# An order of TensorE's work searched anew, with six planning constants and two buffer counts changed

## The chip, the core and the metric

The kernel runs on one core of a Trainium2 chip. A core has a matmul engine (TensorE, PE in the profile, its weight loads shown apart as PEld), a vector engine (VectorE, DVE), an activation engine (ScalarE, ACT), a general one (GpSimd, POOL) and one that issues transfers (SyncE, SP). They run side by side and wait for each other through semaphores. PE writes its results into PSUM, which has eight banks of 128 x 512 fp32 values; VectorE or ScalarE must read a bank out before PE may fill it again. The metric is the time of one execution on the device, in microseconds (us); less is better.

## What is computed

```python
def reference(A_x, A_wq, A_wk, A_wv, A_wo, B_x, B_w_gate, B_w_up, B_w_down, gate_w):
    def _A_ref(x, wq, wk, wv, wo):
        q = (x @ wq).reshape(B, S, H, Dh).transpose(0, 2, 1, 3)
        k, v = x @ wk, x @ wv
        scores = jnp.einsum("bhqd,bkd->bhqk", q, k) * (Dh ** -0.5)
        o = jnp.einsum("bhqk,bkd->bhqd", _softmax(scores), v)
        return o.transpose(0, 2, 1, 3).reshape(B, S, H * Dh) @ wo
    def _B_ref(x, w_gate, w_up, w_down):
        return (_sigmoid(x @ w_gate) * (x @ w_up)) @ w_down
    x = A_x
    g = _sigmoid((x * gate_w).sum(-1, keepdims=True))
    return g * _A_ref(x, ...) + (1 - g) * _B_ref(x, ...)
```

S is 2048 positions, D 512, 32 heads of 16 that share one key and one value head, F 1792. Everything is fp32; products that need the accuracy are made from a high and a low part of each operand, three matmuls for one.

## The kernel before

The 2048 queries are four blocks of 512. A *unit* is four heads of one block: 32 units. For each unit PE computes scores twice. First for the largest score of every query (`maximum`, L1139, code m): the result fills a bank and VectorE reduces it to its maximum (L1141). When a unit's maxima are done, they are turned by a small matmul (T, `max_turn`, L998) and sent into spare rows of the query tile, so that the second computation of the scores (`scores`, L1148, code s) comes out with the maximum taken off; ScalarE takes the exponential (L1150) into a tile `p`. Four such tiles are a *chunk* of 128 keys, and `pv` (L1012, code V) multiplies them with the values into a bank that gathers the unit's sums. The gated layer and the output projections are filled in between, as *fills* (`fill`, L1113, code f): gate, up and down products of the four blocks, then the projection of the attention's results.

Scores and fills contract over 64 rows or fewer, so PE runs two of them at once, one on each half of the array: a *step* is such a pair. V, T and the first projections (G, `project`, L870) use PE in another shape, so the work is a row of steps with *visits* to the other shape between them.

What PE does, in which order, is written out in the string `ORDER` (L683 to L728). Each letter is one code, taken by `State.step` (L657). `V`, `G` and `T` are as above. A hexadecimal digit is a step: its upper two bits say what the upper half gets, its lower two what the lower half gets (0 nothing, 1 a maximum, 2 a score, 3 a fill), so `f` is two fills, `5` two maxima, `b` a score and a fill, `c` a fill alone. A dot issues nothing; it lets the plan's clock run by 25 units. `plan()` (L731) walks through the string and lists all instructions of all engines in order; nothing of its clock reaches the chip, but it decides which engine takes which result, when transfers are issued, and which bank each product gets.

`State` books costs in units. A step is 100, a chunk `VALUES` = 371, a change into the other shape `IN`, out of it `OUT`. A bank that VectorE reads is booked as free `LATE` (until VectorE can begin) + `RED` (a reduction) + `TAIL` + `FREE` units after its matmul (`issue_m`, L514); one that ScalarE reads, `LATE_A` + `EXP` + `TAIL_A` + `FREE_A` (`issue_s`, L524). `take` (L189) hands out the bank that has been free longest and demands that it is free by the plan's clock. At the end of a visit inside a unit the sums' bank is copied out by ScalarE (`finish`, L1016); the first copy of a unit stays, later ones are added to it by GpSimd (`add_sums`, L1025).

`PB` is the number of `p` tiles (2 KB per partition each; the plan lets no more than `PB` wait for their chunk, `can_s`, L509, though `step` itself doesn't ask), `DB` that of tiles for split down weights and output weights (`wd`, 4 KB per partition each, two for one transferred pair). GpSimd splits them (L771, L772) as soon as a pair is free.

After the string comes a fixed end (L1169 to L1197): the last unit's sums are copied out, turned, divided, turned back, multiplied by the last output weights and stored.

Of the kernel before, what the change touches and what calls it, by code (L numbers as in the profile page):

```python
# [118 lines left out]
class State:  # L121
# [559 lines left out]


ORDER = (  # L683
    "GGGGGGG555G55G555.G55........5G55GG555GGG555G55G555GG55G557G777fddfffdffdfd7GT7dffff7ffd75Gdefffdfe7edef6f6f9fbf"
    "7b7b7bbdfedef97bf9fbffeeaaVV555VVV7b7b7bfbdedbdbf9fededededbf7bfb76fef67effd9VVVV5b7b7bfbfe7eeddbf6fedeedef7f6fe"
    "7bdbdbf6fbf5VTVV555VVVV7b7bb7fedbdbde7bfededeedef7e7fedb7bbd7bffd6V569VV97fbdbb7f9fe7ef6fbdededee7fb7f6f9fb7edef"
    "f75VVV59aVV97fbe7dbfbdbf6f9fbdededee7fe7f9f9fbdffd7775VVTVV655VVV76fef97efedee7f6f9fb7b7bbdfdbfb7edbdbfefed5VV56"
    "6VVV5bfbf97bf6fbf9f9fededeedef77e7bfb7be7ffddd5VVVV7b7bb7b7fededef9fe7edeede7ff6f9fe7e7bf9fbfaTV5a5VVVV5bbb77fef"
    "9fbdef6dbfedeede7f7efe7edb7eff7775VV599VV595VVV5eeedfbdf6fb7edbfbdb7bb7bdff97bfef9fe7edfd5VV566VVVdededefe7e7e7b"
    "dbfb7b7b7bbdfedf6feedf9ff7775VTVV596VV9dfbf6bdfb7bdbf9ef7ededee7ff6fed6febffb7bb9V555VVVVV5e9ffef6fbdef6e7bdfb7b"  # L690
    "7bbdfedfb79feed7bffd6V695VV569VV5a5VTVdedeedfe7e7e7bbdfb7b7b7bbfddbfbd6fede7efbfaV599VV5bb7fbb7fe7eedf9f6fededee"
    "f7b7fed6fe7dfd7777VVV599VV5ededefefb7e7e7bfbdb7b7bbdfedf9fbede7ff75f5VVVV966V5efeedbfb77b7bfedbddd7TVV999V9b77bf"
    "fededeedb7fefbb5VV566VV695VV5bfbf6f9f6fbde7b7efededee7fedbf76fbbdbfdbf5VV659TVV5eedfe7bfe7bf6dedbfb7b7bbfdf6f9f9"
    "fef6fedf75VVVVVVV7b7bbddef9fb7e7efbdeeeded7ffe7bf6fede7b7f5bV995VV5bbfbd7efb7bdef9fe7ededee7ff6fbdb7ebdf7ff56VVV"
    "TVVde5eefbdfb7afd7bfed7b7bbbfd7bedf6fedefb7fd6V595VVVVV7bdef9f6fb7ef97bfbdedeede7f7bf6f9fee7fbdbfaV5aaVV569VV959"
    "VV97bfb7f6f9feb7defe7edeede7ff6bfde7efb5bffa7TVV59aVVVVVV5efbf6defedb7b7edefb7bb7bfdf9fb7bdeedf6ff5dVVV5bb7bfb7f"
    "bd6fef9fededeeddfb7bbf76fef6fbfee6V9a9VV5a9VVVV5b7bbfefdb7af7defbdedeede7fb7f6fb7bf6fed9fdV555VVTVV97b7bff6f9fb7"
    "eedf6fedeede7ff67bfedefe7f7776VV999VVVV9dfeed7bfb7eededfb7b7b7bbdfedfb79fef6def7f5VVV555VVVdedeedfe7e7bf97efb7bb"
    "7b7bdf7bfb7b7eeeddfdddVTVVV5bbfdbf6f9fb7bf9efdeddeedbfb7b7fe7e7beffed5VVVV7b7b7bfededb7bf9fedededee7f7bf6fbb7f6d"
    "effd5VVV566VV5eefdef6fbdbf97ef9fb7b7bbfddbfe7b7bdefedbddTVV665VV569VV5b7bbff6fedef97bf6fdedeeef77efbde7bf9fe77d7"  # L700
    "VVVVVV5efededbfb7ef9f6fe7b7b7bbfddeedf9fef9fb7bfaV569VV699VVV5bb7fef6fede7ededbfb7bb7bfd7ebdf6fef9fbdfe5V566VV95"
    "6TVV595VVV79b7bfdef9fb7be7fededeedef77ee7f9fbbdf6fbfaV656VVV5efedbf9f9fbf6f6edfb7bb7bfdf9efde7bb7fdfdd5VV665VVVT"
    "V7b7bdbdef6fbf9edbf7ededee7ff67bfedefefb797bVVVdedefe7b7b7b7bfbdeefd5VV6ddefefb7b7b7bf9fefed9VVVVVV7b7edbdbfe7ed"
# [543 lines left out]
```

## Time and profile before

| | |
|---|---|
| median of 3 runs | 1588.13 us (1587.35 to 1588.98) |
| the profiled execution, its own time | 1589.17 us |
| its span, first to last instruction | 1587.0 us |
| mean granted TensorE clock | 0.999 |
| reductions on VectorE (L1141) | 2048, 1256.0 us busy |
| exponentials on ScalarE (L1150) | 2048, 1035.4 us busy |
| splits and additions on GpSimd, all | 788.7 us busy |
| bytes moved | 102.04 MB, mean 64 GB/s |

Rows of groups give line, engine, operation, output and inputs, shapes and the count, then the busy time, the mean length of one in ns, and the idle time of the engine before them with what ended it. Rows of the timeline and of the chain give the start and the length in us; neighbouring instructions of one kind are merged, so a length covers all of them. Matmuls overlap, so their starts tell more than their lengths. Each V leaves eight records on L1012: four matmuls, each shown twice.

### The profile page before, as it was taken

The page shows a single profiled execution, that of the slowest core. Times are in us where ns is not written, and L with a number is a line of the kernel's source. Part 1 is how long each engine was busy: PE and PEld are TensorE (multiplying, and loading weights), DVE is VectorE, ACT ScalarE, POOL GpSimd, SP SyncE. Part 2 cuts the span into 40 slices and gives each one's busy share as a digit, 9 for nine tenths or more (in the row PEclk, how much of TensorE's full clock was granted, in tenths as well). Part 3 has the DMA queues.
Part 4 walks back from the last instruction along what each step waited for, and adds up shares of the span by engine and source line. Part 5 has one row for each costly group of instructions (what it writes and reads, how often), then busy time and mean ns, then how long its engine had stood idle before and what let it go on. Part 6 is the DMA issues. An engine that isn't in the chain of part 4 may idle for free.

```text
span 1587.0 us, 33642 instructions
## 1 busy us (share of the span) xinstructions
PE 1578.4 (99%) x12950; PEld 1026.2 (65%) x12950; DVE 1357.7 (86%) x2320; ACT 1233.2 (78%) x2426; POOL 788.7 (50%) x662
## 2 busy tenths in 40 slices
PE   9999999999999999999999999999999999999998
PEld 7776666666666566666656666666666666676663
DVE  6989999999888889898998889888998988888751
ACT  4277787888778877887877978888887877787887
POOL 4253373657363455376463537274726346436432
PEclk9999999999999999999999999999999999999999
DMA  7422021122021221122121212022212122112011
GB/s 248 159 80 65 25 78 31 50 78 79 25 78 39 82 75 52 34 72 65 43 75 41 80 50 83 27 63 65 78 35 75 39 75 78 52 35 62 15 35 51
DMA packets 56000, 102.04 MB, mean 64 GB/s; under 512 B 16612, under 2 KB 18148, under 8 KB 55840
## 3 DMA queue, kind: packets, MB, share of 16 engines
q1 hardware_dynamic: 55840, 99.89, 20.3%
q8 instruction: 102, 1.67, 0.5%
q14 instruction: 58, 0.48, 0.1%
HBM read 78.11 MB, written 21.22 MB: 63 GB/s over the span
## 4 chain that ended last, share of the span: by engine, by line
PE 95%; ACT 3%; DVE 1%; SPq 0%; DMA 0%; issue 0%; POOL 0%; DVEq 0%; ACTq 0%
PE bank L1113 32%; PE bank L1012 29%; PE bank L1139 17%; PE bank L1148 14%; PE bank L870 3%; ACT p L1150 2%; SPq L986 0%; PE bank L998 0%; DVE mx L1141 0%; PE bank L1191 0%; DMA qs<-qd 0%; ACT x L796 0%; DVE x L802 0%; DMA wkv_raw<-wkv 0%; ACT q L965 0%
## 5 line engine op out<-in xcount | busy, mean ns | idle before, releaser
L1141 DVE TENSOR_REDUCE mx<-bank 128x1 f32<-128x512 f32 x2048 | 1256.0, 683 | 163.1 <-PE bank L1139 136.5
L1150 ACT ACTIVATE p<-bank 128x512 f32<-128x512 f32 x2048 | 1035.4, 665 | 4.9 <-PE bank L1148 1.0
L1148 PE MATMUL bank<-qs,ks 64*128 64x512 f32 x2048 | 725.8, 396 | 0.0
L1139 PE MATMUL bank<-ks,qs 62*128 62x512 f32 x2048 | 674.6, 409 | 0.2 <-DMA qs<-qd 0.2
L1012 PE MATMUL bank<-p,v_aug 128*32 128x512 f32 x4096 | 486.7, 597 | 0.3 <-ACT p L1150 0.3
L1139 PEld LDWEIGHTS bank<-ks,qs 62*128 62x128 f32 x2048 | 334.5, 184 | 152.7 <-issue 51.9
L1148 PEld LDWEIGHTS bank<-qs,ks 64*128 64x128 f32 x2048 | 361.9, 185 | 77.1 <-ACT p L1150 31.2
L1026 POOL TENSOR_TENSOR ou<-ou,ou 128x512 f32<-128x512 f32 x181 | 233.3, 1290 | 283.8 <-ACT ou L1019 277.2
L1019 ACT COPY ou<-bank 128x512 f32<-128x512 f32 x212 | 129.7, 612 | 279.4 <-PE bank L1012 136.5
L1113 PE MATMUL bank<-x,wu 64*128 64x512 f32 x1344 | 272.1, 391 | 0.3 <-SPq L1117 0.3
L1012 PEld LDWEIGHTS bank<-p,v_aug 128*32 128x32 f32 x4096 | 122.4, 109 | 230.1 <-issue 192.4
L1113 PE MATMUL bank<-wd,hl 64*128 64x512 f32 x1344 | 271.0, 391 | 0.0
L1113 PE MATMUL bank<-x,wg 64*128 64x512 f32 x1344 | 269.2, 391 | 0.0
L1113 PEld LDWEIGHTS bank<-x,wu 64*128 64x128 f32 x1344 | 201.5, 185 | 18.3 <-issue 1.7
L1113 PEld LDWEIGHTS bank<-wd,hl 64*128 64x128 f32 x1344 | 200.3, 185 | 17.0 <-issue 0.8
L1113 PEld LDWEIGHTS bank<-x,wg 64*128 64x128 f32 x1344 | 199.4, 185 | 16.8 <-issue 1.2
L845 POOL CAST wg<-rg 128x1024 fp32r<-128x1024 f32 x27 | 28.1, 1039 | 137.8 <-PE bank L1113 64.2
L1092 POOL TENSOR_TENSOR ba<-ba,pa_d 128x512 f32<-128x512 f32 x29 | 36.8, 1282 | 83.8 <-ACT pa_d L1089 83.8
L845 POOL CAST wu<-ru 128x1024 fp32r<-128x1024 f32 x27 | 28.1, 1041 | 97.8 <-PE bank L1113 58.1
L772 POOL TENSOR_TENSOR wd<-rd,wd 128x512 fp32r<-128x512 f32 x56 | 72.3, 1291 | 4.5
L772 POOL TENSOR_TENSOR hl<-h,hl 128x512 fp32r<-128x512 f32 x56 | 72.0, 1286 | 4.5
L1113 PE MATMUL bank<-wa,o 64*128 64x512 f32 x360 | 70.0, 392 | 0.0
(82 smaller groups left out, 758.4 us busy)
## 6 DMA issues: line engine op xcount, KB each, us to landing
rg<-wg SPq DMA_DIRECT2D x28, 512.0 KB
ru<-wu SPq DMA_DIRECT2D x28, 512.0 KB
rd<-wd SPq DMA_DIRECT2D x28, 512.0 KB
qs<-qd SPq DMA_DIRECT2D x192, 64.0 KB
qd<-q SPq DMA_DIRECT2D x32, 256.0 KB
od<-ou SPq DMA_DIRECT2D x31, 256.0 KB
xf<-x_in SPq DMA_DIRECT2D x16, 256.0 KB
ra<-wo SPq DMA_DIRECT2D x8, 512.0 KB
```

What stands on the lines that cost most here:

```text
L772: lo.tensor_tensor(hl[:, 1, :], raw, f32(hl[:, 0, :]), op=ALU.subtract)
L845: nc.gpsimd.tensor_copy(WS[item][:, 0, :], raw)
L870: nc.tensor.matmul(ps, w[:, p, part(kc)], X[b, kc][:, q, :], start=i == 0, stop=i == 3 * KC - 1)
L1012: nc.tensor.matmul(ps[32 * j:32 * j + 32, :], v_aug[:, c, :], PT.pop((u, c, j)), start=start, stop=stop)
L1019: nc.scalar.copy(to, ps)
L1026: nc.gpsimd.tensor_tensor(SUMS[u], SUMS[u], PARTS_OF[u].pop(0), op=ALU.add)
L1092: nc.gpsimd.tensor_tensor(BA[b, t], BA[b, t], PA[b, t].pop(0), op=ALU.add)
L1113: ins = nc.tensor.matmul(banks[i], l, r, start=start, stop=stop)
L1139: nc.tensor.matmul(banks[i], qs_t[u % 3][r, pr, part(qt)], ks[r, kb * 512:(kb + 1) * 512], start=True, stop=True)
L1141: nc.vector.tensor_reduce(MX[u][:, pr, h, qt, kb:kb + 1], banks[i], axis=AX.X, op=ALU.max)
L1148: nc.tensor.matmul(banks[i], ks[r, part(c)], qs_t[u % 3][r, pr, :], start=True, stop=True)
L1150: nc.scalar.activation(p, banks[i], AF.Exp, scale=0.25)
```

## The change

The string `ORDER` is replaced by another, for the same work: 512 V, 32 T, 24 G, and the same number of maxima, scores and fills. Six constants of the plan change, and two numbers of buffers, which together take the same memory as before.

```diff
-RAW, WB, DB, PB, HB, BA_BUFS = 2, 2, 4, 29, 6, 4
+RAW, WB, DB, PB, HB, BA_BUFS = 2, 2, 6, 25, 6, 4
...
-LATE, LATE_A, FREE, FREE_A = 190, 200, 65, 60
+LATE, LATE_A, FREE, FREE_A = 188, 196, 30, 55
...
-RED, GATED, SUM, ENDS, PARTS, INVERSE, LOWER = 260, 258, 285, 60, 225, 70, 285
+RED, GATED, SUM, ENDS, PARTS, INVERSE, LOWER = 258, 258, 285, 60, 225, 70, 285
...
-IN, OUT, VALUES, TURN = 52, 94, 371, 92
+IN, OUT, VALUES, TURN = 52, 106, 371, 92
...
 ORDER = (
-    "GGGGGGG555G55G555.G55........5G55GG555GGG555G55G555GG55G557G777fddfffdffdfd7GT7dffff7ffd75Gdefffdfe7edef6f6f9fbf"
-    "7b7b7bbdfedef97bf9fbffeeaaVV555VVV7b7b7bfbdedbdbf9fededededbf7bfb76fef67effd9VVVV5b7b7bfbfe7eeddbf6fedeedef7f6fe"
...
-    "fddbbfd6fbfbfeede6VaaaTVVVVVVfbbfeffbbfeeeeeeffffffbbffffbaffeabfeVVbbbbffffbfaaVVaaeeVVeeaaVVaaaVVaaaVVa.aaVVaa"
-    "VaaVV...............Vcccccccccccc"
+    "GGGGGGG555G55G555G55.....5.G55GG555G55G555GG55G57fffffdffdff55fG7777fffffffffddd.55GGTG55dGeef7b7eed7ebfdef7b7bb"
+    "7bdbfdbdbb7defbf9ddddVVV7b767bfe7bfedbe7efdedeede77ef7bfafdf6f7fd75VV555VVVVd6ededfbb7fbdef6ef7b7b7bbddefb7e7f6f"
...
+    "bfeedeeeVVVVVV6ddeeef7ef79fedbfb7b7bb7bdfdbf6fbdbbffeeeeaTVVVaaaVVVeaaeVVffbebbfffeabVVeffbfeefbefbbbaVVaaaVVbbbf"
+    "ffebff.eeeeeVaefffebffbbbVaaaVVaaaVVaaaVVeeeccca888VVVVcccccc"
 )
```

Counted over the whole string:

| | before | after |
|---|---|---|
| steps | 4256 | 4264 |
| steps with work on one half only | 12 | 28 |
| unbroken runs of V, G and T | 210 | 196 |
| runs with V in them | 196 | 183 |
| of these with five V or more | 15 | 29 |
| dots | 25 | 45 |
| copies of sums (`finish`) | 212 | 191 |
| additions of copies (`add_sums`) | 181 | 160 |
| most `p` tiles held at once | 29 | 25 |

More of the change, by code (lines that the diff above doesn't have):

```diff
@@ L689 @@
[L689 to L703, printed above, removed]
@@ new lines @@
+    "7bdbfdbdbb7defbf9ddddVVV7b767bfe7bfedbe7efdedeede77ef7bfafdf6f7fd75VV555VVVVd6ededfbb7fbdef6ef7b7b7bbddefb7e7f6f"
+    "bf9ddVTVVGVVbf7bb7bffbdedbdefedbdddeeef7fb7e7bb7fedff5d5VVV7b76efbdbdfb7eb7defededee7f7e6ffbd9fb7fdf57VV955VVVV7"
+    "b7b7b7bfededef9fe7ededee7bfd6fdefb7ebf7f57TVV955VVV977bfedbdbf6fef9fede7b4bbd7bfbdfb7afdeffede.55VVV659VV977bfbd"
+    "ebf76fbdbefded.6ceed7bf6fbbdf6ff6fe7f55VV555VVVVd9edeedeff7bb9f7e7fb7bb7bfddefedef6f97bf7f5VTVVV9b77fbdbbfdedb7e"
+    "fbdededee77fb7e.b7eed7fbffd516VV655VVVdedeeddef6f6fb7bfb7b7b7bbdfdbdbfbd6fef6ff5dV659VVVVV6dedeedf7bfaf9f77efb7b"
@@ new lines @@
+    "7bbdbdfe7fbdbbde7edf5c5.VV666VTVVVdedee5efb7fedbf6fb7b7bb7bddbf9fdbfebd7e.eef71aVV6a5VVVV5ededeeedffb7b7bfe7b7b7"
+    "bbdedfdefed6fb7bff7ddeeedddVTVVVV5eef7bb77bfb7b7bb7fbdbf9dbff6edeffe.6aV995VV655VVV977bbfdbbdfe7bf6defedeeddbbf7"
+    "b77bf6fbdedffb7b7e777VVVVV9dedfef9bfdedeeddef6fbb7b7ff6f97e.edbeVVV6a6VTV956VV5edefbfd7b7bbbfdbfdee6VV699V97bb7f"
+    "fedededeb7e7ff57VVVded6fe7ebfd6f6fb7efbb7b7b7f9fedf9fafdfed5f7VVVVV5ededeeffb76fbdefb7b7b7bbddfebf9fb5fefffd55VV"
+    "TVV6deeeddfbf76fb7efe7b7b7bbdfedbdfaf6fdf7dd77VV555VVVdede7eeb7fdbf9e7ef7b7bb7bfddebfde7bdeb7fefaV956VVVVVdedeed"
@@ new lines @@
+    "edf6fb7b7efb7b7b7b7bff9dbfbdef67fe7f6fdbb77bVTVVV9d9ffeedfbdedededefe76fef9f7ebf7bf9b.5VV696V59aV56aVV965VVVdede"
+    "edef7b7bbd7efe7b7bb7bfdf9defb7edef6ff5bV969V69aVV659VVV977bbfdbfbd6fbf6fedededee7ff6fe7edbf7fd7775VTVVV9edfedb7f"
+    "ed9faf7f9fb7bb7bdbf7defee6fdef7f75VVVVV9ddebf7bfbd6fbb7bfdeddeeef77ef6f9fbdbfff755VVVV5eeeddfefb76fefe7b7b7b7b7f"
+    "ededefafdbdfb7f97TV9a5V99aVVVVV6ddedefb7ef6fee7bf7b7b7bbddef9ff6fafdf9fbfbb77b777VVVVV5bdefbdefededeededfb7bb7f6"
+    "dfe7bffdda.6VVV655VVVdedeedfb79fbdbf9f9fb7b7b7efbf7e7bf6fefeded6VTV965VVV6ddeeff6fb7ed6fefb7b77bbbdfdbdedefee7e7"
@@ new lines @@
+    "ffdedffd9d5VVVVV6de7bf7bfb7b7bb7b7f9fafdbddfb6fffd6.5dVV656VV996V56aV5edeeedff6feb7f9fb7b7b7bbddeffbdbdbe7f6eef5"
+    "35.VTVV96aVVVVdedeedede7fb7bf6fb7b7bb7bdfdedef6fef97ebffef9dedddVVVVV56fefb7bfb7b7bb77.bf9fedbdb7bf6fdfded5VV656"
+    "VTVV6eddeef7fb79fee7bdfb7bb7bdfdb9fb7fbf6ebdffe7b7b77dVVVVV9defbdf6edfedededef6f.b76fbdefb7b7dfe6VV9a5V555VVV6de"
+    "eedf7fbd6faf7f9fb7b7b7bfdedbdbfaf7edff5dVVVV5b7bbffedededef6fbfb76TVVVV977bfbdfededee7f6ff797VV9de9ff7ee7f6fbf9f"
+    "edb7bb7bddfb7eefdb7bf6def5.c5VV6a5VVVV7b9fdeb7bfdedb7be7fededeedf7bf67efbf9fbf6f9V696VTVVVVdededeedfe76fbb7fb7b7"
@@ new lines @@
+    "bb7bdefdf9f6fbed7eff7b7bb77bbVVVVV79bfdededefededeedfe76fbdeff9fb7bfba.6VV96aVV5a5VVV95effef9bf7bb7dbbdfeedde.de"
+    "def6f7eefb77b7f771aVV655VVTV9dedfbe7fed6fe7efb7b7b7bbddfbbddefbf6f9dbf9V56eVV565VVVVdededefe7b7ef6e7fb7b77bbbfde"
+    "dfed9fbbdfa7fd7V95aV65aV995VV656VV6dfeed7eef79fbf9f6fb7bb7bdff9f6fbdb7edbdffb77b7f76VTVVV5bfbdeedfedededeedf6fb7"
+    "eedf6fbf7f77.95VVVVV6dededfef9f6fb7bef7b7b7bbdfdef9edfeb7fd7f75VV599VVVV97bf7bdedefb7bf9fe7edeede7f7ef6dbfbf97ef"
+    "f69TV69bVVVVV6ededdedfefb7e7bbf7b7b7bbdfedb7fedeed7ebffefeddd5dVVVV67b7fb7efe7bb77bb7fed9fedefdbf9ff775.9VV596VV"
@@ new lines @@
+    "VTV977bfbdebfd6feb7f9fedeede7f6f6fbdf9fb7bfefb7b7bb7bVVVVV59fefef9fededeeddefb7ef67bff9e7fe7f5.5VVVVV597b.fefede"
+    "fe79fedbfb7b7b7ebdf9fbbdf7beddefd46VV655VVV6deededef7fbf6b7f9fbb77bbdfdbfbdef6f6dbfee9TVVVV579VV5b7bb7fedef9f6fb"
+    "7efdeeeddf6fee7fede7bb7effdedef9f5VVVVV65fbbf7bfbdb7b7bb7fbdef9db7fedefbdf5.5VV656VV666V999V5eeedf7e7ef9fe7efb7b"
+    "7bb7bdfdbfbdbdedbf6eff5TVVVVVV97bfdb7ebf79fafdf6fedeede7ff6e7fbdef9f6ffdbdededf5VVVVV676ffb7efb7b7b7b7bf9febdedd"
+    "fbdbf6fb.9eVVV699V556VV6b7fdbfbdeededfaf6f777VVVdedeef7b7bb77bedf9ff5dVTVdededee77efb7b7bdefb7bb7bddfbf6bfdb7ef9"
@@ new lines @@
+    "edfdV695VV666V59aVVVde5eef7ee7fedbf9b7fb7b7b7f9fefed9fefadf7fb5VVVVV6ddedeef7bf6fe7efb7b7bb7bdfdef9def9fef6f7fed"
+    "9fdedeVTVVVde7e7bb7fb7b7bb7b7f9fedbb7fdbdefefe5.5VVV565VVV5edebfdefb7edb7ef9fb7bb7bdf6fedfb76feedff751.aVTV995VV"
+    "56aVVVde6def7bfe7bdbf6fedb7b7bbdbdfbd.6fefdef6bbfac6VV5a9V596VVVV7b97bbff9fd6fef9fe7ededeef77ee7fedbb7f9ff79V699"
+    "V6a6VVVVV9edef7f6edfedefb7b7bb77bbdfdefbdbde7efff575TVVVVde5eedefb7fedaf7fb7b7b7bbdbfdf9fede7eb7fef519.VVV566VVV"
+    "97b7efeddefe7bf9fedb7bb7bdedfb7fed6fbdbbcd5f.6VV655VVV95fbbf7bf9f6fb7eefdedededbf7b7bf6fe7eedfb15f5.VTVVVV7b7bb6"
@@ new lines @@
+    "fddefbb7bdfededdeeef77be7f6feedfef6fedbdfd5VVVVV67bbfd7ebfdb7bb7b7.bdfbdbe7dbfe7edffd6.6V955VVVVV5eedfbf6e7fedbf"
+    "9f6f.b7b7bbdfbd6fefdb7ebdfefa1aVTVVVVV6dedef7e7bf9fbb77bfedeede7ff69fe7f9fbe7bdf5VV579VVV69edffe7ef7ede7bef7b7b7"
+    "bbddfbdef9fbf6f9ff5dV695VVV695VTV7b7b79bfdbfafd7efededee.de7bf76fef7bdbb7eefac5VV596VVVV5ededefe7bf9fef6bf7b7bb7"
+    "bdedfed7efedbe7bffefed9dddVVVV56effb7bfb7b7b7bb7fedbf9b7bfddeffdd6.5VV656VV59aTVVV67b6fff9efdbdb7bbfdedeede77fb7"
+    "bfb7bbddeeffbfb7b767VVVVV97feedbdfededeededf6fb7e7efedfb7b7d7.9VV596VVVVdedededeef7e7b7bfb7b7bb7bddfebdb7feedfe7"
@@ L728 @@
+    "6fbVTV996V595VVV797bbffddedeeef7fbfba9V569VV977bfedeef76..be77fbe.def9VV695VV677bb7bff9fbd9fefedededee7b7fb7fb7b"
+    "bfeedeeeVVVVVV6ddeeef7ef79fedbfb7b7bb7bdfdbf6fbdbbffeeeeaTVVVaaaVVVeaaeVVffbebbfffeabVVeffbfeefefbbbaVVaaaVVbbbf"
+    "ffebff.eeeeeVaefffebffbbbVaaaVVaaaVVaaaVVeeeccca888VVVVcccccc"
 )
```

25 lines of the change are left out of this document (removed).

## The prediction

> **What bounds the kernel now.** I read the busy times and the chain of waits on the page first.
>
> ```profile
> span 1587.0 us, 33642 instructions
> ...
> PE 1578.4 (99%) x12950; PEld 1026.2 (65%) x12950; DVE 1357.7 (86%) x2320; ACT 1233.2 (78%) x2426; POOL 788.7 (50%) x662
> ...
> PE 95%; ACT 3%; DVE 1%; SPq 0%; DMA 0%; issue 0%; POOL 0%; DVEq 0%; ACTq 0%
> PE bank L1113 32%; PE bank L1012 29%; PE bank L1139 17%; PE bank L1148 14%; PE bank L870 3%; ACT p L1150 2%; SPq L986 0%; PE bank L998 0%; DVE mx L1141 0%; PE bank L1191 0%; DMA qs<-qd 0%; ACT x L796 0%; DVE x L802 0%; DMA wkv_raw<-wkv 0%; ACT q L965 0%
> ```
>
> PE is never idle and 95% of the chain is PE: the span is the sum of what PE is told to do, in the order of the string. So the change is priced by what the new string makes PE do, and by what waits it adds. The next question is what one code costs. I read that from the chain in order of time and from the timeline of PE (start, length, what).
>
> ```profile
> 284.80 0.99 PE bank L1012 x8
> 285.80 0.95 PE bank L1139 x6
> 286.75 4.43 PE bank L1012 x40
> 291.18 0.43 PE bank L1139 x2
> ...
> 487.95 5.29 PE bank L1012 x48
> ```
>
> ```profile
> 1541.59 1.56 PE L1113 MATMUL bank<-wa,o 64*128 64x512 f32 x12
> 1542.95 0.39 PE L1148 MATMUL bank<-qs,ks 64*128 64x512 f32 x1
> ...
> 1557.47 1.92 PE L1012 MATMUL bank<-p,v_aug 128*32 128x512 f32 x16
> 1559.32 0.96 PE L1148 MATMUL bank<-qs,ks 64*128 64x512 f32 x6
> 1560.21 0.64 PE L1012 MATMUL bank<-p,v_aug 128*32 128x512 f32 x4
> ```
>
> A **values chunk** (V) leaves eight matmul records, so x40 is five chunks and x48 six: one more costs 5.29 - 4.43 = 0.86 us. A **step** is a pair of matmuls on the two halves of the array: six steps took 1542.95 - 1541.59 = 1.36, so 0.227 each where nothing disturbs. The upper end comes from the chain: L1113, L1139 and L1148 hold 63% of 1587.0, which over 4256 steps is 0.235. I take 0.231.
>
> A **switch**, from steps to values and back, is what is left over. From 285.80 to 291.18 lie three steps and one visit of five chunks: 5.38 - 3 x 0.231 - 5 x 0.86 = 0.39. From 1557.47 to 1560.21 lie two chunks and three steps: 2.74 - 1.72 - 0.69 = 0.33. I take 0.36, the middle.
>
> **The change, part by part.** I counted both strings letter by letter.
>
> *Switches.* Unbroken runs of V, G and T fall from 210 to 196 (runs with values in them from 196 to 183): 14 x 0.36 = **-5.0 us**, with ends of -4.6 and -5.5. The chunks themselves stay at 512.
>
> [...]
>
> *Steps.* 4256 become 4264, because 28 codes give work to one half only where 12 did; the matmuls are the same (2048 maxima, 2048 scores, 4404 fills). 8 x 0.231 = **+1.85 us**.
>
> *Dots.* A dot issues nothing; it stands where the plan expects PE to wait. There were 25 and will be 45. What the old ones cost shows in two places of the timeline:
>
> ```profile
> 31.72 0.97 PE L1139 MATMUL bank<-ks,qs 62*128 62x512 f32 x6
> 32.62 3.01 PE L870 MATMUL bank<-x,wq 128*128 128x512 f32 x12
> 35.56 1.17 PE L1139 MATMUL bank<-ks,qs 62*128 62x512 f32 x6
> 36.84 3.02 PE L870 MATMUL bank<-x,wq 128*128 128x512 f32 x12
> ```
>
> ```profile
> 1570.02 1.92 PE L1012 MATMUL bank<-p,v_aug 128*32 128x512 f32 x16
> 1572.27 1.55 PE L1012 MATMUL bank<-p,v_aug 128*32 128x512 f32 x8 [0.34 <-ACT p L1150]
> ...
> 1573.75 3.03 PE L1113 MATMUL bank<-we,o 64*128 64x512 f32 x12
> ```
>
> The three steps at 35.56 have eight dots among them and take 1.28 until the next group, those at 31.72 only 0.90, though one dot follows them: eight dots cost 0.38, one costs nothing. Before the last chunk stand fifteen: it should begin at 1570.02 + 1.72 = 1571.74, begins at 1572.27, and its own 1.48 is 0.49 over the 0.99 of a lone chunk; 1.02 in all. The new tail has no dots, and six remain at the start: -1.02 - 0.38 + 6 x 0.047 = -1.1. The other 39 are spread one by one; a single dot above cost nothing, a full one 1.02 / 15 = 0.068, so 0 to 2.7, of which I take 1.0, nearer the row with one dot. Net **-0.1**, from -1.1 to +1.6.
>
> *A bank sooner free.* `FREE` falls by 35 units and `LATE`, `RED` by 2 each. A chunk is 371 units and 0.86 us, so a unit is 2.32 ns and FREE alone is 81 ns: the plan now hands out a bank that much closer behind VectorE's reduction. What is late next, if it isn't free, is PE's weight load (waits are carried there), and everything queued behind it on PE.
>
> ```profile
> L1141 DVE TENSOR_REDUCE mx<-bank x2048: 627/682/694, 25.1 to 1531.3; 128x1 f32<-128x512 f32 x187
> ...
>   PEld bank L1139: 18.5, 27
>   PEld bank L1012: 6.7, 22
>   PEld bank L1148: 5.4, 8
> ```
>
> ```profile
> 380.48 2.48 DVE L1141 TENSOR_REDUCE mx<-bank 128x1 f32<-128x512 f32 x4
> ...
> 381.81 0.18 PEld L1139 LDWEIGHTS bank<-ks,qs 62*128 62x128 f32 x1
> ...
> 381.50 0.39 PE L1139 MATMUL bank<-ks,qs 62*128 62x512 f32 x1
> ...
> 381.73 0.39 PE L1148 MATMUL bank<-qs,ks 64*128 64x512 f32 x1
> ...
> 381.96 0.40 PE L1139 MATMUL bank<-ks,qs 62*128 62x512 f32 x1
> ```
>
> Four reductions in 2.48 with 0.68 for the last run 0.60 apart, so the second ended at 380.48 + 0.60 + 0.68 = 381.76. The load it released began 0.05 later, at 381.81, and its matmul at 381.96: 0.23 after the one before, as always. A load can follow the reduction's end by 0.05 and PE still loses nothing. The three groups above are 57 loads out of 2048 reductions that were held by one at all. If each held load now costs the whole 81 ns: 4.6. If the slack takes it: 0. I take **+2.5**, the middle, since the new plan places its codes 81 ns closer throughout, so that more loads than these 57 come near their bank.
>
> *ScalarE's constants* (`LATE_A` -4, `FREE_A` -5 units: 21 ns) have the same answer at a quarter of the size; the 2.5 includes them. The larger `OUT` emits nothing; it only shifts what the plan thinks is ready.
>
> *Fewer visits, fewer copies.* Each visit that ends inside a unit hands its sums to ScalarE, and all but the first to GpSimd. By the string these fall from 212 to 191 and from 181 to 160.
>
> ```profile
> L1019 ACT COPY ou<-bank 128x512 f32<-128x512 f32 x212 | 129.7, 612 | 279.4 <-PE bank L1012 136.5 <-issue 61.6 <-POOL hl L771 17.9
> ...
> L1026 POOL TENSOR_TENSOR ou<-ou,ou 128x512 f32<-128x512 f32 x181 | 233.3, 1290 | 283.8 <-ACT ou L1019 277.2 <-PE bank L1113 2.3 <-DMA qs<-mt 2.0
> ...
> PEld bank L1113 <- POOL wd L771: 0.8, 1, 0.8
> ```
>
> That is 21 x 0.612 = 13 us of ScalarE and 21 x 1.29 = 27 us of GpSimd less, worth nothing by itself: both sat idle for some 280 us before these very instructions, under PE's matmuls.
>
> *Buffers.* The third pair of down weights lets GpSimd split sooner; fills waited once, 0.8 us, for such a split, so 0, at best -0.8. The four tiles of `p` given up for it bind in the string itself, which never holds more than 25; a score's exponential writes a tile that an earlier chunk on the same PE queue has already read, so no new wait: 0. SP issues the same transfers, with more time before the fills need them.
>
> *The tail.* Behind the last V stand six single fills instead of twelve (counted among the steps).
>
> ```profile
> 1574.75 1.38 ACT L1089 ACTIVATE pa_e<-bank,gsig 128x512 f32<-128x512 f32 x2 [2.04 <-PE bank L1113]
> ...
> 1576.03 0.64 ACT L1175 COPY ou_last<-bank 128x256 f32<-128x256 f32 x2
> ...
> 1576.71 0.66 PE L1177 MATMUL bank<-consts,ou_last 128*128 128x128 f32 x4
> ```
>
> ScalarE scales two fills' results (0.69 each) ahead of copying the last sums, and the transposes wait for that copy. With six fills PE is at the transposes 1.4 us sooner, and one such scaling can stand in the way: 0 to 0.7, I take **+0.3**.
>
> **Sum:** -5.0 + 1.85 - 0.1 + 2.5 + 0.3 = -0.45 us on a span of 1587.0. That execution took 1589.17, 2.17 more than its span; the three timed runs have a median of 1588.13, so I put the difference on the median: **1587.7 us**, no change that can be told. Its own range, one or two terms off: 1585.0 to 1591.0.
>
> **The rivals.**
> (A) *The saving arrives whole*: no held load costs PE anything, single dots stay free. -5.0 + 1.85 - 1.1 = -4.3: 1583.8. For it speaks the load of 381.81; against it that the plan now spends 81 ns of the slack that this load had.
> (B) *Slower: the bank isn't free sooner.* The place is PE's weight load behind a reduction or an exponential. Before, reductions held 57 loads and exponentials the ones in these rows:
>
> ```profile
> PEld bank L1139 <- ACT p L1150: 33.9, 57, 0.8
> PEld bank L1148 <- ACT p L1150: 31.2, 76, 0.8
> ```
>
> together 190. A plan 81 ns too early would show once in each stretch between visits, since a late PE stays late until the next: 183 x 0.081 = 14.8. It decides from about 8 us of loss on, net of the rest: half of it, 7.4, gives -5.0 + 1.85 - 0.1 + 7.4 + 0.3 = +4.5, 1592.6; all of it 1600. Against it: so far most held loads cost no step.
> (C) *The change doesn't save what it books*: most of the 0.36 belongs not to the switch but to waits that come back in longer visits (five chunks or more: 15 before, 29 after). If only the slow start of the first step belongs to it (at 1559.32 three steps begin within 0.96 - 0.39 = 0.57 where two pitches make 0.46: 0.11), 14 save 1.5, and the sum is +3.05: 1591.2. Against it: a lone chunk takes 0.99, five 4.43, six 5.29, each 0.13 over its chunks, whatever the length. [...]
>
> **How the numbers follow.** Forecast 0.53, A 0.20, B 0.20, C 0.07. About 0.2%, 3.2 us, is what a measurement here can tell from no change. A falls below (0.20); the forecast and half of C inside (0.56); B and the other half above (0.24). The range goes from below A, 1583.3, to just beyond B's half price, 1593.0; outside it lie the rest of B (0.1) and an A without any dots' cost and with a dearer switch (under 0.1).
>
> **What would show it.** In the profile after: span 1586 to 1587; 191 copies on L1019 and 160 additions on L1026; the last chunk 0.99 long with no wait; L1113, L1139, L1148 and L1012 with the same busy time to within 3 us; 60 to 150 loads held by a reduction, most 0.1 or less. A shows as a span near 1583 with held loads as few as now. B shows as three or more times the loads held by `DVE mx`, and steps of 0.26 and more in the middle of stretches. C shows as switches of 0.36 and over, or longer ones behind visits of five. The forecast is wrong if the span moves by over 3 us, or if something that this text calls covered (GpSimd's splits, the `p` tiles, SP) ends PE's waits.

## The result and the profile after

The changed kernel takes **1594.14 us** (median of 5 runs, 1593.14 to 1595.23), the kernel before 1588.13: a ratio of 1.0036, 95% interval 1.0025 to 1.0047. It is slower by 6 us. The forecast was 1587.7 with a range up to 1593.0, so the time lies outside, on the side of rival B. The profiled execution took 1595.23, its span 1593.5.

The page of the changed kernel, first and fourth part:

```profile
span 1593.5 us, 33670 instructions
...
PE 1583.6 (99%) x12950; PEld 1040.4 (65%) x12950; DVE 1345.3 (84%) x2311; ACT 1223.7 (77%) x2414; POOL 772.9 (49%) x650
...
PE 98%; DVE 1%; ACT 0%; SPq 0%; DMA 0%; issue 0%; POOL 0%; DVEq 0%; ACTq 0%
```

VectorE has 12.4 us less to do than before, ScalarE 9.5 and GpSimd 15.8, and the kernel is slower all the same: 98% of the chain is PE, which has the same 12950 matmuls. So the time went into the distances between the starts of PE's matmuls. The groups confirm the counts of the prediction, 191 copies and 160 additions:

```profile
L1019 ACT COPY ou<-bank 128x512 f32<-128x512 f32 x191 | 114.9, 602 | 294.1 <-PE bank L1012 194.6
L1026 POOL TENSOR_TENSOR ou<-ou,ou 128x512 f32<-128x512 f32 x160 | 206.3, 1289 | 259.0 <-ACT ou L1019 257.4
```

I laid the string beside the starts of PE's matmuls in both traces and added up the distance from each code to the next:

| kind of distance | before: us, count, mean ns | after: us, count, mean ns |
|---|---|---|
| step to step | 891.17, 3836, 232.3 | 903.49, 3872, 233.3 |
| first step behind a visit | 71.25, 210, 339.3 | 66.73, 196, 340.5 |
| step to the visit behind it (entry) | 73.94, 209, 353.8 | 72.96, 195, 374.2 |
| chunk, another visit code behind it | 276.01, 316, 873.4 | 286.66, 329, 871.3 |
| chunk, a step behind it | 197.12, 196, 1005.7 | 183.74, 183, 1004.0 |
| first projections (G) | 60.75 | 62.75 |
| turns (T) | 0.99 | 0.96 |
| before the first and behind the last code | 15.82 | 16.16 |

From it two sums follow. **Counts at the old means:** 36 plain steps more are +8.36 us, 14 first steps less -4.75, 14 entries less -4.95, 13 exits less (at 1005.7 - 873.4 ns each) -1.72; together **-3.1 us**. **Means at the new counts:** plain steps 3872 x 1.02 ns = +4.0, entries 195 x 20.4 ns = +4.0, first steps +0.2, chunks -1.0, G +2.0, the end +0.3; together **+9.5 us**. By its counts the new order saves what it was made to save. It loses three times as much, and 7.9 of these 9.5 us lie in plain steps and entries that became longer.

What stands behind the longer steps is in the view of one line's instructions that tells who waited for them. Reductions, changed kernel:

```profile
L1141 DVE TENSOR_REDUCE mx<-bank x2048: 624/680/693, 26.8 to 1533.5; 128x1 f32<-128x512 f32 x187
...
  PEld bank L1139: 30.3, 56
  PEld bank L1148: 15.7, 50
  PEld bank L1012: 8.8, 27
```

Exponentials, the kernel before and the changed one:

```profile
L1150 ACT ACTIVATE p<-bank x2048: 590/657/942, 84.6 to 1571.8; 128x512 f32<-128x512 f32 x187
...
  PEld bank L1139: 33.9, 57
  PEld bank L1148: 31.2, 76
  PEld bank L1012: 8.4, 23
```

```profile
L1150 ACT ACTIVATE p<-bank x2048: 588/642/1092, 83.8 to 1579.0; 128x512 f32<-128x512 f32 x187
...
  PEld bank L1139: 22.8, 46
  PEld bank L1012: 20.0, 68
  PEld bank L1148: 17.7, 46
```

Over all rows of weight loads in these views, loads held by a reduction rise from 68 to 145, by an exponential from 158 to 171: 226 to 316. Steps and entries lost 7.9 us; over 90 more held loads that is 88 ns each, about the 81 ns by which the plan hands out a bank sooner. This is a quotient, not a price: reckoned in the same way against the kernel before, three more runs of the new order (new_m432, new_loose and new_oldconst, below) give 57, 80 and 122 ns. The views also leave out short waits: the late load of the example below, with 0.08 us of idle time before it in the trace, is not among them.

A late bank shows in two ways. Some steps become long as a whole: plain steps of 260 ns or more were 54 before and are 137 now, and what they take beyond 232.3 ns each rose from 3.2 to 8.4 us, more than the 4.0 us that the plain steps lost in all. Ahead of half of them (68, 17 before) a load began within 0.1 us of the end of a reduction that it waited for, ahead of 27 (16 before) within 0.1 us of an exponential's. Other steps have one half alone delayed, which shows as no gap between steps. Steps whose second half starts over 100 ns behind the first were 35 before and are 245 now. One of them, from the timeline of the changed kernel (start, length, what; neighbours are merged):

```profile
611.33 2.48 DVE L1141 TENSOR_REDUCE mx<-bank 128x1 f32<-128x512 f32 x4
...
612.31 0.54 PEld L1139 LDWEIGHTS bank<-ks,qs 62*128 62x128 f32 x3
...
612.54 0.63 PE L1139 MATMUL bank<-ks,qs 62*128 62x512 f32 x3
...
613.10 1.06 PE L1012 MATMUL bank<-p,v_aug 128*32 128x512 f32 x8
```

The step ahead of the visit is two maxima. Four reductions of 0.68 in 2.48 run 0.60 apart, so the second ends at 612.61; the held load follows and its matmul, the last of the three, starts at 612.54 + 0.63 - 0.39 = 612.78. The step's first half, the second of these three matmuls, had started at 612.59 in the trace, 0.19 sooner. The visit starts at 613.10, 0.32 behind the late half and 0.51 behind the first, where the mean before was 0.354. So it is over all entries: from the first half to the later one the mean was 22 ns before and is 36 now, from the later one to the visit 331 and 338. The halves stay over 100 ns apart for up to 21 steps in a row, and the visit starts behind the later one, so some 14 of the 20 ns that an entry lost are this drift.

Last, the end. PE, then ScalarE, in the changed kernel:

```profile
1581.20 1.66 PE L1113 MATMUL bank<-we,o 64*128 64x512 f32 x6
1583.90 0.71 PE L1177 MATMUL bank<-consts,ou_last 128*128 128x128 f32 x4 [1.04 <-ACT ou_last L1175]
1585.02 0.77 PE L1186 MATMUL bank<-consts,on 128*128 128x128 f32 x2 [0.41 <-DVE on L1184]
```

```profile
1582.20 1.38 ACT L1089 ACTIVATE pa_e<-bank,gsig 128x512 f32<-128x512 f32 x2 [2.11 <-PE bank L1113]
1583.48 0.64 ACT L1175 COPY ou_last<-bank 128x256 f32<-128x256 f32 x2
```

PE is through with the six lone fills while ScalarE still scales two results; the copy of the last sums stands behind both scalings, and PE is idle for 1.04 us. Twelve fills covered that before.

### The profile page after: what moved, and what is told of

It is laid out like the page before. It is cut to its first block, busy times and chain, and to the rows that moved or that the text cites. A ratio compares the mean times of both kernels' runs of the same rounds, so it can differ in the third digit from the quotient of the medians.

```text
span 1593.5 us, 33670 instructions
## 1 busy us (share of the span) xinstructions
PE 1583.6 (99%) x12950; PEld 1040.4 (65%) x12950; DVE 1345.3 (84%) x2311; ACT 1223.7 (77%) x2414; POOL 772.9 (49%) x650
## 4 chain that ended last, share of the span: by engine, by line
PE 98%; DVE 1%; ACT 0%; SPq 0%; DMA 0%; issue 0%; POOL 0%; DVEq 0%; ACTq 0%
PE bank L1113 33%; PE bank L1012 29%; PE bank L1139 17%; PE bank L1148 15%; PE bank L870 3%; PE bank L998 0%; SPq L986 0%; DVE mx L1141 0%; DMA qs<-qd 0%; ACT x L796 0%; DVE x L802 0%; DMA wkv_raw<-wkv 0%; PE bank L943 0%; POOL wkv_s L772 0%; DVE ba L1195 0%
## 5 line engine op out<-in xcount | busy, mean ns | idle before, releaser
L1019 ACT COPY ou<-bank 128x512 f32<-128x512 f32 x191 | 114.9, 602 | 294.1 <-PE bank L1012 194.6
L1026 POOL TENSOR_TENSOR ou<-ou,ou 128x512 f32<-128x512 f32 x160 | 206.3, 1289 | 259.0 <-ACT ou L1019 257.4
L1113 PE MATMUL bank<-x,wu 64*128 64x512 f32 x1344 | 284.8, 393 | 0.0
L1113 PE MATMUL bank<-x,wg 64*128 64x512 f32 x1344 | 278.1, 392 | 0.0
L1113 PE MATMUL bank<-wd,hl 64*128 64x512 f32 x1344 | 277.8, 392 | 0.0
L1012 PEld LDWEIGHTS bank<-p,v_aug 128*32 128x32 f32 x4096 | 126.7, 109 | 228.0 <-issue 169.8
L1113 PEld LDWEIGHTS bank<-wd,hl 64*128 64x128 f32 x1344 | 204.1, 185 | 17.2 <-issue 2.5
L1092 POOL TENSOR_TENSOR ba<-ba,pa_d 128x512 f32<-128x512 f32 x32 | 40.8, 1285 | 99.8 <-ACT pa_d L1089 88.9
```

The costliest lines, as they stand in the source:

```text
L1012: nc.tensor.matmul(ps[32 * j:32 * j + 32, :], v_aug[:, c, :], PT.pop((u, c, j)), start=start, stop=stop)
L1019: nc.scalar.copy(to, ps)
L1026: nc.gpsimd.tensor_tensor(SUMS[u], SUMS[u], PARTS_OF[u].pop(0), op=ALU.add)
L1092: nc.gpsimd.tensor_tensor(BA[b, t], BA[b, t], PA[b, t].pop(0), op=ALU.add)
L1113: ins = nc.tensor.matmul(banks[i], l, r, start=start, stop=stop)
```

## The experiments

Fifteen kernels, each compared with the kernel before on the same chip (its median there 1588.04 to 1588.67). A kernel called old has the order of before, one called new the changed kernel's; a number in a name is that of the columns left in.

**1. Reductions trimmed, in both orders.** If banks come too late behind VectorE, a shorter reduction must heal the new order and do little for the old one. Four kernels, 432 and 352 columns of 512:

```diff
-        nc.vector.tensor_reduce(MX[u][:, pr, h, qt, kb:kb + 1], banks[i], axis=AX.X, op=ALU.max)
+        nc.vector.tensor_reduce(MX[u][:, pr, h, qt, kb:kb + 1], banks[i][:, :432], axis=AX.X, op=ALU.max)
```

> The new order; each reduction reads 432 of the 512 columns of its bank (80 of 512 keys are left out of the maxima), so that every bank behind VectorE comes free about 80 ns sooner, as much as FREE was lowered (81 ns). Theory 1, the bank behind VectorE is not free when the new plan says so: most of the 6.0 us come back, 1588 to 1590. Theory 2, ScalarE and the entries into the visits are what is late: 1592.5 or more. [...]

> The old order with the same shortened reductions. Theory 1: its banks were nearly always free in time, so at most 1.5 us come back: 1586.5 to 1588; the gap between the orders shrinks from 6.0 to 0 to 2.5 us. [...]

> The new order, reductions of 352 of 512 columns (160 of 512 keys left out of the maxima): banks behind VectorE free some 165 ns sooner. Theory 1: no wait behind VectorE is left, and what remains is the order's own work, 2.9 us less than the old order's by the counts, plus the other waits: 1585 to 1588. [...]

> The old order, reductions of 352 of 512 columns. Theory 1: 1585.5 to 1587.5, and the new order now at or below the old one (gap -2 to +1). [...]

**2. Exponentials trimmed, in both orders**, alone (s432) and with the reductions (ms432). The 80 columns left out of a `p` tile keep what an earlier tile left there; so that this is data and not unwritten memory, the `p` tiles come from a fixed ring:

```diff
-        p = PT[u, c, 2 * pr + h] = ap.tile([P, 512], F32, tag="p", name=f"p{u}_{c}_{pr}_{h}", bufs=PB)
-        nc.scalar.activation(p, banks[i], AF.Exp, scale=0.25)
+        p = PT[u, c, 2 * pr + h] = p_tile()
+        nc.scalar.activation(p[:, :432], banks[i][:, :432], AF.Exp, scale=0.25)
```

> The new order; each exponential takes 432 of the 512 columns (80 of 512 queries of every block are left out of the attention), so it ends about 65 ns sooner; the p tiles are one fixed ring instead of a pool. Theory 2, the rest of the loss is visits that begin before ScalarE has the last exponentials, and banks behind ScalarE: 3 to 5 us come back, 1589 to 1591, and the step before a visit falls from 374 ns to 345 to 358. Theory 1 alone, the bank behind VectorE and nothing else: at most 1 us comes back, 1593 or more, and that step stays at 368 or more.

> The old order with the same shortened exponentials and ring. Theory 2: 1 to 2 us come back (its end waits for exponentials, 1.0 us, and its visits somewhat), 1586 to 1587; the gap between the orders falls from 6.0 to 3.0 to 4.5. Theory 1 alone: the gap stays at 5 or more.

> The new order, reductions and exponentials both at 432 of 512 columns. If the two waits and the longer end (11.0 against 9.7 us behind the last code) are all of it: the order's own work, 2.9 us less than the old one's, is left with the end's +1.3: 1583.5 to 1586. If a third thing is behind it: 1587.5 or more.

> The old order, both at 432 of 512 columns. If the two waits and the end are all of the loss: 1585 to 1586.5, and the new order now stands 0 to 2.5 us below it. If a third thing is behind it: the new order stays above it by 1.5 or more.

Measured, with the ratio to the kernel before and its interval, and the loads held by a reduction and by an exponential:

| trimmed | old order, us | new order, us | new - old | held, old | held, new |
|---|---|---|---|---|---|
| nothing | 1588.13 | 1594.14 (1.0036, 1.0025 to 1.0047) | +6.0 | 68 + 158 | 145 + 171 |
| reductions, 432 | 1586.39 (0.9987, 0.9978 to 0.9996) | 1588.99 (1.0002, 0.9993 to 1.001) | +2.6 | 59 + 169 | 67 + 202 |
| reductions, 352 | 1586.40 (0.9986, 0.9977 to 0.9995) | 1588.46 (1.0002, 0.9993 to 1.001) | +2.1 | 75 + 167 | 57 + 203 |
| exponentials, 432 | 1591.81 (1.0015, 1.0006 to 1.0024) | 1598.61 (1.0062, 1.0049 to 1.0075) | +6.8 | 83 + 62 | 190 + 97 |
| both, 432 | 1589.06 (1.0003, 0.9993 to 1.0012) | 1587.23 (0.9992, 0.9983 to 1.0) | -1.8 | 70 + 63 | 63 + 108 |

The kernels with the ring have chunks that take 4 to 5 us more in all: in the old order a chunk grew from 873.4 to 879.3 ns and one with a step behind it from 1005.7 to 1020.0. No run has the ring without the trimming, so which of the two does it isn't shown. So the last two rows are read across, not down.

Several times came out higher than was expected by the theory that holds: new_m352 (at most 1588) and its gap (at most +1), old_s432 by 4.8 us, old_ms432 by 2.6 and new_ms432 by 1.2. The longer chunks explain the last three in part.

Reading the gaps: reductions that end 82 ns sooner take 3.4 us off the gap. Another 74 ns add nothing that can be told. In the trace of new_m432 the loads behind a reduction are back at the old number, and more stand behind an exponential:

```profile
  PEld bank L1139: 24.4, 32
  PEld bank L1148: 5.2, 7
  PEld bank L1012: 4.6, 16
```

```profile
  PEld bank L1139: 27.1, 65
  PEld bank L1012: 23.3, 70
  PEld bank L1148: 20.1, 58
```

(The first fence is the view of its reductions, the second that of its exponentials.) Shorter exponentials alone (532 ns in the middle in new_ms432, where it was 657 in the old order and 642 in the new) do nothing for the gap: the reductions then hold 190 loads. But with the reductions out of the way they take off another 4.4 us (some 0.7 of it may be the chunks, which grew by 4.7 us in the old order and by 4.0 in the new), and the new order is the faster one. What remains, -1.8 us, is near what the counts give (-3.1) plus the longer end (about 1), but it is partly luck that it is: in the two traces the entries of the new order still take 368 ns against 351, 3.4 us in all, and its plain steps are 1.0 ns shorter, which gives 3.8 back. So most of the loss is PE's wait for banks, behind VectorE first and behind ScalarE next, and with that taken away the saving of the switches shows.

The rival reading, that visits wait for exponentials not yet made, does not carry the loss. With trimmed exponentials alone the entries of the new order took 381 ns, not less than 374. The loads of chunks that an exponential held did rise, from 23 to 68, but from the later half of the last step to the visit the mean rose by 6.5 ns alone, 1.3 us over all entries.

**3. The constants apart from the order.** With the string fixed, the constants choose banks and engines only. old_newconst has the old string, the old buffers and the new constants; new_oldconst the reverse, where `take` gives out the bank that is free first even when the plan holds it for not yet free.

```diff
-LATE, LATE_A, FREE, FREE_A = 190, 200, 65, 60
+LATE, LATE_A, FREE, FREE_A = 188, 196, 30, 55
```

> The old order and the old buffers with the change's constants alone: a bank taken as free 30 ticks behind VectorE and 55 behind ScalarE, and the other changed durations. With a fixed order they change only which bank and which engine the plan picks for a step. Theory P, the constants do harm only through the order that was searched under them: 1588.1 within 0.8, and weight loads held by a reduction as before (27 of line 1139, 5 of line 1148), within 30 in all. Rival Q, the banks themselves are chosen so much tighter that the loads are held: 1590 to 1594, and more than 80 loads held by a reduction.

> The new order and buffers, but the plan's choice of banks and engines goes by the constants of before (a bank free 65 ticks behind VectorE and 60 behind ScalarE). Where the order comes back to VectorE's work sooner than those constants allow, the bank that is free first is taken all the same. Theory P, the order is what comes back too soon, and no choice of banks helps: 1593 to 1596, more than 80 weight loads held by a reduction, and a mean offset between the halves of a step of 29 to 33 ns. Rival Q, the choice of banks is the cost: 1588 to 1590.5, under 60 loads held, offset 22 to 26 ns.

old_newconst: 1589.5 us, ratio 1.001 (1.0001 to 1.0019), loads held 75 + 171. new_oldconst: 1598.69 us, ratio 1.0064 (1.0051 to 1.0077), loads held 128 + 185, halves 32 ns apart in the mean (32 in the changed kernel, 23 before). Both missed their expected times on the high side, but in direction they agree: the constants alone do little harm, and the new order isn't healed by the old ones. So the loss lies in where the string puts its codes. What old_newconst lost is not in its body: in the profile its last code begins at 1575.62 (before: 1576.40), and what lies behind that takes 11.53 us (10.65). PE's timeline at its end:

```profile
1576.94 0.63 PE L1177 MATMUL bank<-consts,ou_last 128*128 128x128 f32 x4 [0.94 <-DVE ba L1070]
```

The constants also moved one of the last results to VectorE, and the transposes now wait for that addition. Why new_oldconst is 4.6 us slower than the changed kernel, its one profile tells in part. Its plain steps took 906.2 us against 903.5: two of them, at 1247.3 and 1249.1, took 2.1 us more than a plain step does, and there PE waited for GpSimd to split the attention's result (`o`). The end took 1.2 us more: its last eight products ran for 3.32 us against 1.99, at a granted clock of 0.59 against 1.00. Neither has to do with banks.

**4. The end.** new_copy copies the last sums first; old_filled also puts four of the old order's lone fills ahead of the last chunk, where PE waited, and the transposes behind four of the remaining eight.

```diff
-    for what, *args in plan():
+    todo = plan()
+    last_v = max(n for n, a in enumerate(todo) if a[0] == "values")
+    for n, (what, *args) in enumerate(todo):
         acts[what](*args)
-        if what == "values":
+        if n == last_v:
             end = args[-1]
...
+            for i in range(2):
+                nc.scalar.copy(ou[i], banks[end][:, i * 2 * P:(i + 1) * 2 * P])
```

```diff
-    "VaaVV...............Vcccccccccccc"
+    "VaaVVccccVcccccccc"
```

> The new order, whose last sums are copied out of their bank by ScalarE right behind the last values step, ahead of the two scalings of the output's parts that stood before those copies. In the profile of the changed kernel the first transpose waited 1.04 us for the first copy, which had waited for both scalings. Theory T1, the end behind the last values step costs the new order about 1.0 us because six lone fills cover less than those copies need: the wait of the first transpose falls from 1.04 to at most 0.2 us, the span behind the last values step shortens by 0.6 to 1.0 us, and the time falls from 1594.1 to 1593.1 to 1593.5. Rival T2, the scalings stand on the chain as well (the last sums wait for them anyway): the wait moves behind to the last additions, and the time stays at 1594.1 within 0.4.

> The old order to the last step but 13: four of the twelve lone fills behind the last values step go ahead of it, where TensorE waited 1.0 us for the last exponentials; behind it the copies of the last sums come first, and their transposes stand behind four of the eight fills that are left. Nothing else differs from the kernel before. T1, the order's end is a chain of its own that an order can cover: the wait before the last values step falls by four fills (about 0.9 us) and the reciprocal and the product of the last sums run beside the last four fills; 1588.1 falls to 1586.0 to 1587.2. T2, the end is set by the exponentials and the copies whatever TensorE does between: 1587.8 to 1588.6. Either way a time under 1587.2 would be the fastest of the kernels without a trimmed reduction.

new_copy: 1593.03 us, ratio 1.0031 (1.0019 to 1.0042), 1.1 less than the changed kernel, though the two intervals overlap. Its PE no longer waits before the first transposes, but for 0.41 before the second pair and for 0.51 further on, before the last result is turned back:

```profile
1580.77 1.67 PE L1113 MATMUL bank<-we,o 64*128 64x512 f32 x6
1582.37 0.44 PE L1179 MATMUL bank<-consts,ou_last 128*128 128x128 f32 x2
1583.22 0.44 PE L1179 MATMUL bank<-consts,ou_last 128*128 128x128 f32 x2 [0.41 <-ACT pa_e L1089]
```

old_filled: **1587.10 us**, ratio 0.9995 (0.9986 to 1.0004), and in its end PE runs through to the last products, before which it waits 0.25:

```profile
1571.74 1.21 PE L1113 MATMUL bank<-we,o 64*128 64x512 f32 x4
1572.88 1.06 PE L1012 MATMUL bank<-p,v_aug 128*32 128x512 f32 x8
1573.88 1.19 PE L1113 MATMUL bank<-we,o 64*128 64x512 f32 x4
1575.00 0.66 PE L1182 MATMUL bank<-consts,ou_last 128*128 128x128 f32 x4
```

What lies behind the last code takes 8.32 us; it took 10.65 before, and 9.69 in old_m432, whose granted clock stayed at 1.00 through its last products. Of that difference a part is only moved, since the transposes now stand ahead of four fills. In both orders the traces show the wait gone, and the medians fall by about 1 us, as was expected of a chain at the end; by the times alone the old order's gain is not clear of no change.

**5. The new order loosened, with all its work.** A local search exchanged neighbouring steps, under a plan that takes a bank as free 65 units behind VectorE and 60 behind ScalarE, as before the change. The number of visits stayed.

```diff
-LATE, LATE_A, FREE, FREE_A = 188, 196, 30, 55
+LATE, LATE_A, FREE, FREE_A = 188, 196, 65, 60
...
-    "GGGGGGG555G55G555G55.....5.G55GG555G55G555GG55G57fffffdffdff55fG7777fffffffffddd.55GGTG55dGeef7b7eed7ebfdef7b7bb"
+    "GGGGGGG555G55G555.G55.5......G55GG555G55GG555..G55Gff7ff57fddd7ffdf.G777..fffff7ff7fd5dd.dGGTG555Gefbed7bfe7efe7"
```

> The new order with nothing left out and the same 191 visits of values and turns, but neighbouring steps exchanged by a local search under a plan that takes a bank as free only 65 ticks behind VectorE and 60 behind ScalarE (the change: 30 and 55). Under that rule the plan's own clock counts 682772 ticks for the new order and 680952 for this one; at 233 ns for 100 ticks, as steps took in the trace, that is 4.2 us. Theory P, the change loses its time because its order comes back too soon to banks behind VectorE: 1590.0 to 1592.0, under 100 weight loads held by a reduction (144 in the changed kernel), steps whose second half starts over 100 ns after the first down from 245 to under 150. Rival Q, the loss has another cause (late exponentials, the shape of the runs of values): 1593.5 to 1595.5, whatever the loads do.

> new_loose with the last sums copied out first, as in new_copy, which took 1.1 us off. If the two terms are separate, this is new_loose less 0.8 to 1.2 us, so 1589.0 to 1591.0 by theory P. If the end and the body share a cause, it is new_loose within 0.4 us.

> old_filled (1587.1 us) with its order loosened by the same search under the same 65 and 60 ticks: the plan's clock falls from 680694 to 680181 ticks, 1.2 us at 233 ns for 100 ticks. Theory P, the old order's banks have slack already, so little is left to win: 1586.0 to 1587.3. Rival R, the local search wins by itself, whatever the order: 1583 to 1585, as large a gain as in new_loose.

new_loose: 1594.81 us, ratio 1.0035 (1.0023 to 1.0047): no gain, where 1590 to 1592 was expected. That is the time of the rival Q, but the run can't decide for it, because the loads and the late halves stayed too (221 of over 100 ns, where under 150 were expected). The views of its reductions and of its exponentials say why (its lines are one further down):

```profile
  PEld bank L1140: 21.9, 39
  PEld bank L1149: 11.3, 28
  PEld bank L1013: 9.8, 30
```

```profile
  PEld bank L1140: 25.6, 67
  PEld bank L1149: 23.4, 75
  PEld bank L1013: 19.1, 62
```

Loads held by a reduction fell from 145 to 115, those held by an exponential rose from 171 to 212: 327 in all against 316. The entries got cheaper (363 ns for 374, 2.1 us), the plain steps dearer by 2.3 us. The exchange moved held loads from one engine to the other and removed none; exchanges between neighbours, at least those of this search, do not give the order its distances back. new_loose_copy: 1592.74, ratio 1.0026 (1.0017 to 1.0035), 2.1 less than new_loose where 0.8 to 1.2 was expected; with runs spread over 1592.20 to 1594.70, this says no more than that the end is a term by itself. old_loose_filled: 1587.12, ratio **0.9989 (0.998 to 0.9998)**, against 1587.10 of old_filled: the same search wins nothing here either.

The two filled versions are the fastest that do the whole work: 7 us below the changed kernel, and about 1 us, within 0.05 to 0.11%, below the kernel before; only for old_loose_filled does the interval leave out no change.

## Why the prediction was wrong

*Switches, -5.0: right.* The table gives a switch of the old order as 121.5 ns (entry over a plain step) + 132.3 (exit over a chunk) + 107.0 (first step over a plain one) = 361 ns; 0.36 was taken. Rival C falls: chunks inside the longer visits take 871.3 ns, not more than the 873.4 of before, so no wait came back there.

*Steps, +1.85; dots, -0.1: right as far as seen.* 4264 steps as counted; the last chunk begins with no wait. Counts at the old means give -3.1 us against -3.15 predicted for switches and steps. What the single dots cost can't be told apart from the waits for banks.

***A bank sooner free*, +2.5, between 0 and 4.6: this step failed.** Steps and entries lost 7.9 us. The prediction named the place, and that more loads would come near their bank, and its list of signs gave 60 to 150 loads held by a reduction; 145 it was. The size went wrong twice. The upper end multiplied 81 ns by the 57 loads that were held *before*, though the argument itself said that others would join them: 90 did. Against 81 ns a load the quotient of 88 is close, but with 57 to 122 in other runs that is partly luck. And the sentence that PE loses nothing by a load held to its bank was read from one place where the matmul still had its 0.23. It doesn't hold for the 137 long steps, nor where the other half goes on and the next visit starts behind the late one.

*ScalarE's banks "at a quarter of the size", inside the 2.5: too small.* Experiments 1 and 2 show the two engines one behind the other: heal VectorE's banks and ScalarE's hold PE, 4.4 us between the gaps of m432 and ms432. Here a lateness behind one engine hid that of the other. That ScalarE's two constants caused it, and not the longer runs of steps between visits, no run shows.

*Rival B* had the right mechanism. Its half price, 7.4 us net 1592.6, is close to what was measured; one of its signs was set too high (three times the loads held by reductions; it was 2.1 times), the other came, steps of 0.26 and more: 137 where there were 54. Its argument against itself, that held loads cost no step, was the failed sentence above. It had a chance of 0.20.

*Tail, +0.3, between 0 and 0.7: too small.* It counted one scaling of 0.69 in the way; both stood ahead of the copies. The wait was 1.04, and the median fell by 1.1 when the copies went first.

*Copies, buffers: right as far as seen.* 14.8 us less on ScalarE's copies and 27 on GpSimd's additions bought nothing that shows. For the split of down weights a load waited once, 0.8 us, as before, and no wait for a free `p` tile shows.

Sum with the measured terms, on the spans: -3.1 + 7.9 (steps and entries) + 0.2 - 1.0 (first steps, chunks) + 2.0 (the start, below) + 0.3 (the end) = +6.3, where the two spans differ by 6.4. The end shows as only 0.3 here because the granted clock was 0.50 in part of the old kernel's, where its last eight products took 3.63 us against 1.99 at 1.00:

```profile
1579.00:1582.40 3.40, 3.39 (x8) 0.81 (x6) 1.53 (x3) 0.19 (x1) 0.00 (x0) 0.50 0.07 25
```

(From the windows of the kernel before; the last but two is the granted clock.)

**What stays open:** that PE waits for banks in the new order, and that most of the loss goes with these waits, is shown. Whether the lower `FREE` made the search find such an order, or an order with 14 fewer visits must come back to its banks so soon, is not. Only trimmed work made the new order win.

## To carry to other kernels

When a plan books a resource as free sooner, don't price it by the waits of the profile before: ask how many uses will move up to the new limit, and let the upper end of the term be at least that number times the whole shift. Count the lateness of two engines that share the resource together, since curing one can uncover the other (here the loads held by an exponential rose from 171 to 202 when the reductions were cut to 432 columns), and look at the starts of both halves of a pair and at the next place that needs both, where a late half can be paid (here the visit, whose mean start lay 331 ns behind the later half before and 338 now). And a lower busy time on every other engine says nothing when the distances of one engine's starts set the end (here 12.4, 9.5 and 15.8 us less on the three, and 6 us more in all).

## What the runs showed of the hardware

PE's first projections did not always run at the same pace: the same nine matmuls took 3.40 us in the changed kernel's profile and 2.33 in the old one's.

```profile
7.85 3.40 PE L870 MATMUL bank<-x,wkv_s 128*128 128x512 f32 x9
```

```profile
7.26 2.33 PE L870 MATMUL bank<-x,wkv_s 128*128 128x512 f32 x9
```

(Timelines of the changed kernel and of the kernel before.) It is 2.0 us of the difference between two single traces. Both starts occur with the new order: slow (3.40 to 3.72) in four of its nine profiles, quicker (2.32 to 2.67) in the other five. All eight profiles of the old order are of the quick kind (2.31 to 2.64). So whether the change has a part in it is open, and no run settles what decides it. The windows give a granted clock of 1.00 for this stretch in both, so here the matmuls' own pace tells more than that column. Nor was it expected that with `p` tiles from a fixed ring and trimmed exponentials a chunk would take 4 to 6 ns and one with a step behind it 14 ns more, with the same instructions on PE; this wasn't tried further.
